# FFN chunks of 256 tokens throughout, and matmuls with unused results in TensorE's idle time

## The chip, the cores and the metric

The kernel runs on one core of a Trainium2 chip. The metric is the device time of one execution in microseconds (us). Every comparison is made against runs of the kernel before in the same rounds on the same chip.

## The reference

One transformer block on 2048 tokens of width 1024: layer norm, multi-query attention (32 heads of 32, one shared K and V), residual; layer norm, gated FFN of width 3584, residual.

```python
x = A_x
h = x + A(_layernorm(x))       # q = xn @ wq; k = xn @ wk; v = xn @ wv; softmax(q k^T / sqrt(32)) v @ wo
h2 = h + B(_layernorm(h))      # (sigmoid(hn @ w_gate) * (hn @ w_up)) @ w_down
```

## The kernel before

The program is laid out by a scheduler in Python. It holds a model of the engines' times and decides, instruction by instruction, what TensorE does next. What it decides is a fixed order: each engine is given its own list of instructions, with semaphores to wait on.

Queries are handled in 16 tiles of 128 tokens. A tile has 8 groups of 4 heads, and a group needs 8 exponentials (`exp`, 128x1024) on ScalarE, so there are 64 per tile and 1024 in all. Around them TensorE does the scores (S), the product with V (PV), the output projection (OP), and as filler, where ScalarE is busy, the FFN of an earlier tile: gate and up (GU) and down (D).

```python
CH = [[0], [1]] + [[t, t + 1] for t in range(2, NT, 2)]     # FFN chunks, in tiles: 128, 128, 256, 256, ...
NSLAB = 5                                                  # slabs of weights in flight; one slab = 256 columns of gate and of up
...
def load_slab(s, deps):
    ...
    for w, W in ((0, B_w_gate), (1, B_w_up)):
        ops.append(dma(lambda w=w, W=W: SP.dma_start(
            wgu[:, sl, w, :, :], W[:, pi * SW:(pi + 1) * SW].rearrange("(a p) f -> p a f", p=P)),
            f"sl{sl}{w}", D * SW * 2, deps, prio=4))
...
# GU of one slab: 2 x 8 matmuls for gate, as many for up, n = 128 or 256 columns each
    for f in range(2):
        for dt in range(DT):
            r.append((mm(F_ps[:, b, f * n:(f + 1) * n], wgu[:, sl, w, dt, f * P:(f + 1) * P], hnT[:, dt, 0:n],
                         dt == 0, dt == DT - 1), n, [slab_ld[s][w]] if f == dt == 0 else []))
...
    load_slab(s + NSLAB, [last])                           # after the up matmuls: both loads of a later slab
...
while True:                                                # the scheduler of TensorE
    ...                                                    # S, PV, filler groups, if one can run
    if v == 0 and known([c_id, c_w], t):                   # before the first scores: warm-up matmuls
        pl.op("pe", mm(S_ps[:, 5, :], ident[:, :], hact[:, 0:512], True, True), [c_id, c_w], **t_mm(512))
        continue
    pl.free["pe"] = t + 50.0                               # nothing to do: idle for 50 ns
    idle += 1
```

Each `matmul` becomes two instructions of TensorE, a weight load and a matmul: the profile below counts 24,252 of each.

The softmax here doesn't subtract the row's maximum and nothing guards it: scores larger than these inputs give would overflow.

## Time and profile before

| | before |
|---|---|
| median of the rounds with the change | 1208.87 us (1206.99 to 1213.16, 4 runs) |
| span of the profiled run, mean granted clock | 1204.7 us, 0.978 |
| TensorE / ScalarE busy | 94% / 87% |
| tiles 1, 2, 3 (start of the first exp to start of the next tile's) | 75.7, 72.0, 67.2 us |
| tiles 4 to 15 together | 785.3 us, so 65.4 us each |
| exps end / what is left after them | 1103.3 us / 101.4 us |

The page of the kernel before. Part 1 is busy time; in part 2 the span is cut in 40 slices of 30 us, and a digit is the busy share (or the granted clock) in tenths:

```profile
PE 1136.5 (94%) x24252; PEld 764.4 (63%) x24252; DVE 841.1 (70%) x1553; ACT 1043.2 (87%) x1202; POOL 50.6 (4%) x84
...
PE   9999889889589999999999999999999999999999
...
ACT  6799889889989999999999999999999999996010
...
PEclk9999899999679999999999999999999999999999
DMA  8764797694017551656145631656146622754470
```

The reader sees one long even stretch and a disturbed one in the slices 4 to 11, counted from 0 (120 to 360 us). The same by stretches; the columns are the stretch, its length, busy time of each engine (with instructions), granted clock, DMA share and GB/s:

```profile
130.00:200.00 70.00, 56.66 (x1507) 45.21 (x1507) 44.15 (x83) 58.93 (x73) 0.00 (x0) 0.93 0.93 261
223.00:278.00 55.00, 46.71 (x1236) 37.68 (x1237) 35.39 (x70) 45.61 (x59) 1.24 (x2) 0.97 0.94 250
300.00:342.00 42.00, 25.56 (x792) 17.81 (x782) 28.92 (x54) 38.53 (x42) 2.19 (x3) 0.66 0.07 21
345.00:1100.00 755.00, 740.58 (x16709) 501.00 (x16710) 568.88 (x1024) 729.97 (x823) 23.47 (x33) 1.00 0.49 133
```

The fourth number of busy time is ScalarE. It works 84% of the first stretch and 83% of the second, where the two FFN chunks of 128 tokens run and the DMA share is above 0.9; 92% of the third, where no FFN work is ready; and 97% of the rest. The third stretch, as TensorE's timeline shows it (start, length, what; in brackets the idle time before it and what ended it):

```profile
314.57 0.61 PE L348 MATMUL S_ps<-QTb,kT 32*128 32x128 bf16 x16 [1.43 <-ACT Pr L547]
315.12 1.90 PE L348 MATMUL F_ps<-Pr,Vb 128*32 128x128 bf16 x64
316.80 0.64 PE L348 MATMUL F_ps<-Ts,ones 128*32 128x128 bf16 x16
317.37 0.61 PE L348 MATMUL S_ps<-QTb,kT 32*128 32x128 bf16 x16
```

TensorE waits 1.43 us for ScalarE, its clock is down (0.50 from 313.2 to 326.8 us), and then the 64 PV matmuls take 1.90 us (1.08 at a clock of 1.00, at 560.77 us), so the next scores come late for ScalarE.

### The profile page before, as it was taken

The page shows a single profiled execution, that of the slowest core. Times are in us where ns is not written, and L with a number is a line of the kernel's source. Part 1 is how long each engine was busy: PE and PEld are TensorE (multiplying, and loading weights), DVE is VectorE, ACT ScalarE, POOL GpSimd, SP SyncE. Part 2 cuts the span into 40 slices and gives each one's busy share as a digit, 9 for nine tenths or more (in the row PEclk, how much of TensorE's full clock was granted, in tenths as well). Part 3 has the DMA queues.
Part 4 walks back from the last instruction along what each step waited for, and adds up shares of the span by engine and source line. Part 5 has one row for each costly group of instructions (what it writes and reads, how often), then busy time and mean ns, then how long its engine had stood idle before and what let it go on. Part 6 is the DMA issues. An engine that isn't in the chain of part 4 may idle for free.

```text
span 1204.7 us, 52525 instructions
## 1 busy us (share of the span) xinstructions
PE 1136.5 (94%) x24252; PEld 764.4 (63%) x24252; DVE 841.1 (70%) x1553; ACT 1043.2 (87%) x1202; POOL 50.6 (4%) x84
## 2 busy tenths in 40 slices
PE   9999889889589999999999999999999999999999
PEld 5745575665357765766566755766576756775684
DVE  8677667657667878687867778676877777786211
ACT  6799889889989999999999999999999999996010
POOL 4100000000000000000000000000000000000000
PEclk9999899999679999999999999999999999999999
DMA  8764797694017551656145631656146622754470
GB/s 240 195 203 141 227 277 185 167 274 99 20 48 202 151 138 35 185 143 184 43 129 142 185 101 38 187 144 174 49 123 169 179 69 68 209 144 122 123 209 18
DMA packets 315146, 172.84 MB, mean 143 GB/s; under 512 B 35120, under 2 KB 305456, under 8 KB 314928
## 3 DMA queue, kind: packets, MB, share of 16 engines
q1 hardware_dynamic: 312848, 169.37, 51.8%
q8 instruction: 190, 3.11, 1.1%
q10 hardware_dynamic: 2080, 0.13, 0.1%
q14 instruction: 28, 0.23, 0.1%
HBM read 155.32 MB, written 7.34 MB: 135 GB/s over the span
## 4 chain that ended last, share of the span: by engine, by line
PE 78%; ACT 9%; DVE 6%; issue 3%; POOL 2%; DMA 2%; POOLq 0%; DVEq 0%
PE F_ps L348 65%; PE S_ps L348 13%; ACT Pr L547 8%; DVE Ts L565 2%; DMA hnT<-hn 1%; DVE Oc L610 1%; POOL dsb L308 1%; DVE Oc L608 1%; DVE h_sb L670 1%; DVE st L289 0%; DVE st L291 0%; POOL zb L303 0%; DVE hn L317 0%; POOL rstd L310 0%; DMA zone<-ring 0%
## 5 line engine op out<-in xcount | busy, mean ns | idle before, releaser
L547 ACT ACTIVATE Pr<-S_ps 128x1024 bf16<-128x1024 f32 x1024 | 971.3, 1037 | 52.8 <-PE S_ps L348 51.9
L348 PE MATMUL F_ps<-hnT,ring 128*128 128x256 bf16 (+1 forms) x4032 | 448.1, 263 | 13.9 <-issue 4.6
L348 PEld LDWEIGHTS F_ps<-hnT,ring 128*128 128x128 bf16 x4032 | 342.8, 99 | 79.3 <-issue 19.5
L565 DVE TENSOR_TENSOR Ts<-Pr 128x1024 bf16<-128x1024 bf16 x512 | 341.2, 682 | 9.5 <-ACT Pr L547 5.5
L348 PE MATMUL S_ps<-QTb,kT 32*128 32x128 bf16 x8192 | 212.7, 220 | 31.3 <-ACT Pr L547 22.7
L348 PEld LDWEIGHTS S_ps<-QTb,kT 32*128 32x128 bf16 x8192 | 121.5, 94 | 164.0 <-ACT Pr L547 92.8
L348 PE MATMUL F_ps<-zone,hact 128*128 128x512 bf16 x896 | 218.1, 381 | 0.0
L608 DVE COPY Oc<-F_ps 128x256 f32<-128x256 f32 x128 | 54.2, 423 | 230.7 <-PE F_ps L348 230.7
L565 DVE TENSOR_TENSOR Ts<-Ts 128x1024 bf16<-128x1024 bf16 x256 | 170.5, 666 | 1.4
L348 PE MATMUL F_ps<-Pr,Vb 128*32 128x128 bf16 x8192 | 144.6, 224 | 9.5 <-issue 6.9
L348 PEld LDWEIGHTS F_ps<-Pr,Vb 128*32 128x32 bf16 x8192 | 120.5, 99 | 30.6 <-issue 12.0
L348 PEld LDWEIGHTS F_ps<-zone,hact 128*128 128x128 bf16 x896 | 78.9, 98 | 90.7 <-issue 1.1
L737 ACT ACTIVATE tnh<-F_ps 128x512 f32<-128x512 f32 (+1 forms) x126 | 70.6, 561 | 67.9 <-PE F_ps L348 67.9
L610 DVE RECIPROCAL Oc<-Oc 128x128 f32<-128x128 f32 x128 | 120.9, 945 | 0.1
L741 DVE SCALAR_TENSOR_TENSOR hact<-tnh,F_ps 128x512 bf16<-128x512 f32 (+1 forms) x126 | 77.5, 616 | 59.5 <-PE F_ps L348 57.1
L348 PE MATMUL F_ps<-zone 128*128 128x256 bf16 (+2 forms) x512 | 74.6, 289 | 3.7 <-ACT QTb L235 2.2
L348 PE MATMUL F_ps<-wo_sb,OT 128*128 128x512 bf16 x256 | 65.4, 382 | 0.7 <-DVE OT L612 0.7
L348 PE MATMUL F_ps<-Ts,ones 128*32 128x128 bf16 x2048 | 54.3, 224 | 4.3 <-issue 4.3
L303 POOL TENSOR_SCALAR zb<-mvb 128x1 bf16<-128x1 bf16 (+1 forms) x25 | 10.7, 430 | 1069.1 <-DVE mvb L299 1069.0
L348 PEld LDWEIGHTS F_ps<-zone 128*128 128x128 bf16 x512 | 38.0, 97 | 27.8 <-ACT QTb L235 3.0
L773 DVE SCALAR_TENSOR_TENSOR h_sb<-F_ps,h_sb 128x512 bf16<-128x512 f32 x32 | 21.6, 674 | 30.0 <-PE F_ps L348 29.1
L348 PEld LDWEIGHTS F_ps<-Ts,ones 128*32 128x32 bf16 x2048 | 37.0, 99 | 8.3 <-issue 8.3
(42 smaller groups left out, 275.8 us busy)
## 6 DMA issues: line engine op xcount, KB each, us to landing
ring<-in_B_w_gate_dram SPq DMA_DIRECT2D x126, 512.0 KB, 4.2
ring<-in_B_w_up_dram SPq DMA_DIRECT2D x126, 512.0 KB, 5.5
zone<-in_B_w_down_dram SPq DMA_DIRECT2D x7, 1024.0 KB, 6.9
h_sb<-in_A_x_dram SPq DMA_DIRECT2D x16, 256.0 KB, 2.8
out_dram<-h_sb SPq DMA_DIRECT2D x32, 128.0 KB, 1.7
q_scratch<-hact SPq DMA_DIRECT2D x24, 128.0 KB, 2.9
QTb<-q_scratch SPq DMA_DIRECT2D x6, 512.0 KB, 3.8
ring<-in_A_x_dram SPq DMA_DIRECT2D x5, 512.0 KB, 7.7
```

What stands on the lines that cost most here:

```text
L303: f = pl.op("pool", lambda: POOL.tensor_scalar(out=zb[:, ph, sl].unsqueeze(2), in0=mvb[:, ph, sl, 1:2], scalar1=LN_EPS_BF16, scalar2=None, ...
L308: g = pl.op("pool", lambda: POOL.tensor_tensor(out=dsb[:, ph, sl], in0=zb[:, ph, sl], in1=hb, op=ALU.pow), [f, c0], prio=prio - 1, occ=720 ...
L348: return lambda: PE.matmul(o, lhsT=l, rhs=r, start=start, stop=stop, **kw)
L547: exps[u] = pl.op("act", lambda slot=slot, pb=pb: ACT.activation(out=Pr[:, slot, :].rearrange("p (a b) -> p a b", a=2), in_=S_ps[:, pb:pb ...
L565: return pl.op("dve", lambda: DVE.tensor_tensor(out=out, in0=a, in1=b, op=ALU.add), deps, prio=prio, **t_dve(1024, 1.92))
L608: cp = pl.op("dve", lambda: DVE.tensor_copy(out=Oc[:, k, :], in_=F_ps[:, b, 0:2 * P]), [last, o_ev.get(G - 2)], prio=0, **t_dve(256))
L610: a = pl.op("dve", lambda: DVE.reciprocal(Oc[:, k, P:2 * P], Oc[:, k, P:2 * P]), [cp], prio=2, occ=880, lat=1020)
L670: h_ev[(t, dc)] = pl.op("dve", lambda: DVE.tensor_tensor(out=h_sb[:, t % 4, sl], in0=F_ps[:, b, :], in1=h_sb[:, t % 4, sl], op=ALU.add), [ ...
L737: tanh_of[s] = pl.op("act", lambda: ACT.activation(out=tnh[:, k, 0:2 * n], in_=F_ps[:, b, 0:2 * n], func=ACTF.Tanh, scale=0.5), [last, tn_ ...
L741: e = pl.op("dve", lambda: DVE.scalar_tensor_tensor(out=hactT[:, 2 * pi:2 * pi + 2, 0:n], in0=tnh[:, k, 0:2 * n].rearrange("p (a b) -> p a ...
L773: e = pl.op("dve", lambda: DVE.scalar_tensor_tensor(out=h_sb[:, t % 4, sl], in0=F_ps[:, b, :], scalar=0.5, in1=h_sb[:, t % 4, sl], op0=ALU ...
```

## The change

Its intent: one pass of the gate and up weights instead of two at the start, and no stretch at half clock (37.5 us at 0.50 between 299 and 351 us in the trace of the kernel before). Where the scheduler finds nothing to do after the first scores, it no longer lets 50 ns pass, but issues a 128x256 matmul into a PSUM bank that is free. Nobody reads the result.

```diff
-    CH = [[0], [1]] + [[t, t + 1] for t in range(2, NT, 2)]
+    CH = [[t, t + 1] for t in range(0, NT, 2)]
...
+            idle += 1
+            spare = [b for b in range(2) if known(bank_rel[b], t) and (cur is None or b != cur_b)]
+            if v and spare:
+                pl.op("pe", mm(F_ps[:, spare[0], 0:256], ident[:, :], kT4[:, 0:256], True, True), [k_ev[0]] + list(bank_rel[spare[0]]), **t_mm(256))
+                continue
             pl.free["pe"] = t + 50.0
-            idle += 1
```

## The prediction

> **What bounds the kernel now.** Two regimes, read from the busy time by window and from the starts of the 1024 exp activations (64 per 128-token tile). From 351 to 1100 us ScalarE is busy 725.5 of 749 us and TensorE 734.6: both nearly full; a pair of tiles takes about 131 us (128.6 to 133.7). Before that it is worse: tiles 1, 2, 3 take 75.7, 72.0 and 67.2 us against about 65:
> - 130.5 to 200 and 223 to 278 us: the two 128-token FFN chunks. Each streams all gate and up weights (28 loads of 512 KB) for half the tokens. The DMA share is 0.93 and 0.94 (0.50 later), TensorE waits in program order, and exps come every 1.21 and 1.25 us (1.05 in later FFN stretches, 0.93 when ScalarE alone limits).
> - 300 to 342 us: no FFN work is ready, because chunk 2 needs tiles 2 and 3. TensorE is busy 25.6 of 42 us, the granted clock falls to 0.66, exps come every 0.99 us. In the timeline ScalarE idles 0.77 us per head group, where half-clock PV matmuls (1.90 us instead of 1.08) stand before the next scores. From 342 to 351 us the clock is 0.52 and ScalarE works 7.2 of 9 us.
> - Tail: exps end at 1103 us; the last chunk runs on TensorE alone to 1204 us.
>
> [...] the throttled spans are multiples of 3.41 us at 0.5, about 51 us in all, none between 362 us and the tail.
>
> **What the change does.**
> 1. One 256-token chunk replaces two of 128: one weight pass less (14.7 MB), 448 fewer FFN matmuls with their weight loads, and 14 tanh of 0.60 us instead of 28 of 0.41 (3 us of ScalarE).
> 2. FFN work starts after tile 1 instead of tile 0. The stretch without filler moves from 300-342 us to about 130-190 us.
> 3. In that stretch TensorE has about 40% to spare, so I estimate 200 unused 128x256 matmuls at 0.115 us (17 of that form took 1.96 us). They should hold the clock at 1.0; estimated harm 0 to 2 us.
>
> **On the critical path.** Tile 0 is unchanged and ends at 103 us. By 130 us, 26 exps of tile 1 are done; the other 38 at about 0.95 us end tile 1 near 166 us, 63 us instead of 75.7: gain 12. Tiles 2 and 3 become an ordinary pair, 130.5 instead of 139.2 us: gain 9. Tiles 4 and 5 lose the throttled start: gain 2 to 3. Everything later, and the tail, only shifts. Sum 23: 1187 us, 1.9% faster, at the edge of 2%.
>
> **What would show it right.** Tile 1 ends near 166 us; no DMA share above 0.8 after 60 us; exps every 0.93 to 0.97 us from 130 to 190 us at clock 1.0; exps end near 1080 us; tail still about 101 us. Most of the gain comes from the chunks; the unused matmuls alone are worth 3 to 5 us.
>
> **What would make it wrong.** The unused matmuls delay the scores[...] (exps above 1.0 us there); the clock still drops; the static schedule falls into another order, so pairs take 128 or 134 us (7 pairs: some 20 us either way); or the tail changes, because more or less down-projection is left when exps end (25 us of it now).

What the kernel before does show is a clock of 0.66 where TensorE is busy 25.6 of 42 us, and of 1.00 where it is busy 740.6 of 755; that the unused matmuls "should hold the clock at 1.0" was the author's estimate. The sum: 12 for tile 1, 9 for tiles 2 and 3, 2 to 3 for tiles 4 and 5, so 23.

## More of the kernel before

The same kernel differs by some us from chip to chip: the kernel before had medians of 1203.4, 1205.6 and 1208.9 us in the jobs below. So ratios within a job are what counts, and a few us between jobs mean nothing.

## The result, and the profile after

The changed kernel took 1194.62 us (1193.29 to 1198.72, 4 runs) against 1208.87 us: ratio 0.9883, 95% interval 0.9847 to 0.9919. All ratios here are the mean time of one kernel's fast runs over that of the other's of the same rounds, so not quite the ratio of the medians quoted. In a second job, with 6 runs, it was 0.9872 (0.9844 to 0.9900). It is 14 to 16 us faster; the prediction was 23.

The page of the changed kernel, the same lines:

```profile
PE 1138.6 (95%) x24020; PEld 775.2 (65%) x24141; DVE 843.1 (71%) x1539; ACT 1041.8 (87%) x1188; POOL 50.4 (4%) x84
...
PE   8899899999999999999998899999999999999998
...
ACT  6799899999998999999998999999999999995110
...
PEclk9999999999999999999999999999999999999999
DMA  8765501665155632655054652656155723654470
```

(This trace lacks 121 matmul records, 24,020 against 24,141 weight loads.) The low clock is gone but for two spells of 3.41 us in the trace, at 147.9 and 369.8 us. But the row of ScalarE is not clean: there are eights in slices 12 and 21 (counted from 0), where before had nines. The stretches of the changed kernel:

```profile
130.00:150.00 20.00, 16.76 (x389) 12.26 (x382) 12.52 (x23) 16.26 (x19) 0.00 (x0) 0.95 0.67 232
150.00:190.00 40.00, 39.79 (x940) 29.26 (x941) 27.63 (x49) 38.92 (x43) 0.00 (x0) 0.98 0.05 16
190.00:320.00 130.00, 127.28 (x2996) 88.96 (x3008) 99.80 (x182) 128.51 (x146) 3.54 (x6) 1.00 0.48 129
320.00:1088.00 768.00, 733.47 (x16696) 503.85 (x16770) 577.84 (x1034) 734.11 (x826) 26.02 (x36) 1.00 0.49 132
```

From 150 to 320 us ScalarE works 97 to 99% of the time: this is what was hoped for. From 320 to 1088 us it works 95.6%, where the kernel before had 96.7%. By tiles:

| us | before | after | predicted |
|---|---|---|---|
| tile 1 ends | 178.7 | 170.7 | 166 |
| tile 3 ends | 318.0 | 298.4 | about 296.5 |
| tiles 4 to 15 | 785.3 | 792.9 | about 783 |
| exps end | 1103.3 | 1091.3 | about 1080 |
| after the exps | 101.4 | 101.5 | 101 |

At the end of tile 3 the gain is 19.6 us. Then 7.6 us are given back in tiles 4 to 15, although the work there is the same and the prediction had "Everything later, and the tail, only shifts". The views of waits tell of what kind the loss is. The columns are the engine that waited, what ended the wait, us in total, times, longest us. Before, from 130 to 280 us:

```profile
...
DVE Oc L608 <- PE F_ps L348: 32.6, 15, 4.0
ACT Pr L547 <- PE S_ps L348: 18.6, 19, 2.5
PEld F_ps L348 <- issue: 13.5, 20, 2.5
...
PEld S_ps L348 <- issue: 10.9, 12, 2.3
```

After, from 300 to 1088 us:

```profile
...
PEld S_ps L348 <- issue: 49.6, 189, 2.1
ACT Pr L547 <- PE S_ps L348: 33.0, 53, 2.1
PEld F_ps L348 <- issue: 21.9, 45, 2.2
```

"Issue" means that TensorE stood still and waited for nothing that the profile shows. Most of those waits are short, but a few are of 2 us, and no DMA of weights is on the list in either kernel. One of them in the timeline of the changed kernel:

```profile
367.20 0.39 PE L348 MATMUL F_ps<-hnT,ring 128*128 128x256 bf16 x2
...
367.52 0.40 PE L348 MATMUL S_ps<-QTb,kT 32*128 32x128 bf16 x14
...
369.86 0.29 PE L348 MATMUL S_ps<-QTb,kT 32*128 32x128 bf16 x2 [1.94 <-issue]
...
370.18 1.02 ACT L547 ACTIVATE Pr<-S_ps 128x1024 bf16<-128x1024 f32 x1 [2.13 <-PE S_ps L348]
```

The gap stands inside one block of 16 score matmuls, after the fourteenth. Nothing in the program waits there. ScalarE loses 2.13 us by it, and right after, from 369.8 us on, the clock is at half for 3.41 us.

**What these gaps are.** The trace also has the DMA queue that brings instructions: 189 packets of 16,384 bytes (190 in the kernel before), about as many as TensorE's stream has blocks of 256 instructions: its 48,577 instructions (48,826 before) make 189.8 such blocks (190.7). I call such a block a page. I counted TensorE's instructions in the trace (a pair for each weight load, 24,141 of them, and 295 of semaphores and drains; 24,252 and 322 before) up to each gap over 0.9 us between 130 us and the last exp, from the start of one instruction to that of the next, and looked at what the instruction queue had done:

```
gaps over 0.9 us, 130 us to the last exp     before   after   after, second job
  all                                          30       11       11
  at position 193 or 194 modulo 256            12       10       10      (19.9, 15.6, 14.6 us)
page k starts with packet k-1 landed 1.2 to 1.7 us before (both kernels; the starts with a gap above 0.7 us)
```

Most of the others of the kernel before are waits for ScalarE from 295 to 345 us. So TensorE stands still where its stream crosses from one page of 256 instructions to the next and the page has landed only 1.2 to 1.7 us before. Counting pages and packets, packet k-1 (from 0) was always the one that had just landed when page k started with such a gap, and it had begun to move after page k-1 had started: about one page is fetched ahead. In tiles 4 to 15 of the changed kernel a page lasts 5.8 us on average (3.7 us the shortest), the packet begins to move 1.56 us after the start of the page before (3.8 us at most), it takes 1.13 us (median), and some 1.4 us more pass before TensorE goes on. The sum of the means is 4.1 us, that of the worst case is 6.3 us, more than a page lasts.

By these gaps the two kernels differ as follows (TensorE idle for more than 0.25 us right before position 193 or 194, from one profile each; some expectations below quote other counts of the same gaps): tiles 1 to 3, 16.0 us before and 3.2 after; tiles 4 to 15, 9.7 before and 17.2 after. The last difference, 7.5 us, is the size of the 7.6 us given back. Both vary with the profile: in the second job's profile of the changed kernel, tiles 4 to 15 have 13.6 us of such gaps and take 787.5 us. That is a correlation, and the experiments have to make it a cause.

### The profile page after: what moved, and what is told of

Read it like the earlier page. It is cut to its first block, busy times and chain, and to the rows that moved or that the text cites. A ratio compares the mean times of both kernels' runs of the same rounds, so it can differ in the third digit from the quotient of the medians.

```text
span 1192.8 us, 52074 instructions
## 1 busy us (share of the span) xinstructions
PE 1138.6 (95%) x24020; PEld 775.2 (65%) x24141; DVE 843.1 (71%) x1539; ACT 1041.8 (87%) x1188; POOL 50.4 (4%) x84
## 4 chain that ended last, share of the span: by engine, by line
PE 83%; ACT 6%; DVE 5%; issue 4%; DMA 1%; POOL 1%; SPq 0%; DVEq 0%
PE F_ps L348 70%; PE S_ps L348 13%; ACT Pr L547 5%; DVE Ts L565 1%; DMA hnT<-hn 1%; DVE st L289 1%; DVE st L291 1%; POOL dsb L308 0%; DMA ring<-in_A_x_dram 0%; DVE Oc L610 0%; DVE Oc L608 0%; DVE ring L328 0%; POOL zb L303 0%; ACT ring L332 0%; POOL rstd L310 0%
## 5 line engine op out<-in xcount | busy, mean ns | idle before, releaser
L348 PE MATMUL F_ps<-hnT,ring 128*128 128x256 bf16 x3584 | 441.8, 274 | 9.3 <-issue 4.4
L348 PEld LDWEIGHTS F_ps<-hnT,ring 128*128 128x128 bf16 x3584 | 330.7, 98 | 76.4 <-issue 12.3
L348 PE MATMUL F_ps<-zone,hact 128*128 128x512 bf16 x822 | 199.5, 380 | 6.2 <-issue 5.3
L348 PE MATMUL F_ps<-Pr,Vb 128*32 128x128 bf16 x8192 | 138.7, 220 | 2.1 <-issue 1.3
L348 PEld LDWEIGHTS F_ps<-Pr,Vb 128*32 128x32 bf16 x8192 | 115.8, 97 | 25.1 <-issue 8.1
L737 ACT ACTIVATE tnh<-F_ps 128x512 f32<-128x512 f32 x112 | 67.6, 603 | 65.0 <-PE F_ps L348 64.8
L741 DVE SCALAR_TENSOR_TENSOR hact<-tnh,F_ps 128x512 bf16<-128x512 f32 x112 | 76.0, 678 | 54.7 <-PE F_ps L348 53.5
L348 PE MATMUL F_ps<-zone 128*128 128x256 bf16 (+2 forms) x497 | 71.1, 287 | 5.9 <-ACT QTb L235 2.2
L348 PE MATMUL F_ps<-wo_sb,OT 128*128 128x512 bf16 x227 | 58.7, 381 | 3.1 <-issue 2.5
L348 PE MATMUL F_ps<-kT,ident 128*128 128x256 bf16 x337 | 43.9, 279 | 0.0
```

What stands on the lines that cost most here:

```text
L348: return lambda: PE.matmul(o, lhsT=l, rhs=r, start=start, stop=stop, **kw)
L737: tanh_of[s] = pl.op("act", lambda: ACT.activation(out=tnh[:, k, 0:2 * n], in_=F_ps[:, b, 0:2 * n], func=ACTF.Tanh, scale=0.5), [last, tn_ ...
L741: e = pl.op("dve", lambda: DVE.scalar_tensor_tensor(out=hactT[:, 2 * pi:2 * pi + 2, 0:n], in0=tnh[:, k, 0:2 * n].rearrange("p (a b) -> p a ...
```

## The experiments

**Theory.** A page fetch that waits behind bursts of weight loads comes late, and TensorE stalls. The two small chunks were slow by this, and the change, which shifts every later instruction to another place in its page, met more such stalls in the second part. **Rivals:** TensorE waits for the weights themselves (so the prediction); the unused matmuls get in the way; the new static order is worse.

All 12 runs, with numbers from each run's timed rounds (first three columns) and from its profile (the rest: tiles in us; mean wait from a page's start to the next packet's start in tiles 4 to 15, us; idle time of TensorE above 0.25 us at page starts there, us):

| run | median us | before, same job | ratio (95%) | tiles 1-3 | tiles 4-15 | fetch wait | page gaps |
|---|---|---|---|---|---|---|---|
| before | 1208.87 | | | 214.9 | 785.3 | 1.41 | 9.7 |
| after | 1194.62 | 1208.87 | 0.9883 (0.9847-0.9919) | 195.5 | 792.9 | 1.56 | 17.2 |
| e0_after_again | 1189.89 | 1205.60 | 0.9872 (0.9844-0.9900) | 194.1 | 787.5 | 1.48 | 13.6 |
| e1_chunks_only | 1193.09 | 1203.42 | 0.9910 (0.9865-0.9956) | 205.8 | 783.5 | 1.26 | 8.4 |
| e2_unused_only | 1199.56 | 1203.42 | 0.9978 (0.9930-1.0025) | 207.7 | 780.2 | 1.40 | 8.7 |
| e3_shift_after | 1195.10 | 1203.42 | 0.9929 (0.9882-0.9976) | 196.5 | 785.3 | 1.17 | 12.2 |
| e4_loads_cut_after | 1168.64 | 1203.42 | 0.9715 (0.9676-0.9754) | 195.2 | 767.4 | 0.52 | 0.0 |
| e5_unread_before | 1202.31 | 1205.60 | 0.9970 (0.9928-1.0013) | 210.4 | 785.1 | 1.06 | 6.4 |
| e6_split4_after | 1170.71 | 1205.60 | 0.9710 (0.9684-0.9737) | 195.4 | 767.8 | 0.86 | 0.0 |
| e7_paced_after | 1172.38 | 1205.60 | 0.9729 (0.9702-0.9756) | 194.5 | 771.9 | 1.04 | 1.4 |
| e8_before_split4 | 1184.69 | 1208.93 | 0.9805 (0.9784-0.9826) | 205.7 | 773.0 | 0.85 | 0.4 |
| e8_chunks_split4 | 1172.88 | 1208.93 | 0.9709 (0.9690-0.9729) | 198.1 | 768.9 | 0.89 | 0.5 |
| e8_unused_split4 | 1178.18 | 1208.93 | 0.9758 (0.9733-0.9783) | 203.9 | 767.0 | 0.86 | 0.0 |
| e9_split_all | 1169.49 | 1208.93 | 0.9681 (0.9660-0.9702) | 192.2 | 768.0 | 0.90 | 0.0 |

All results are correct but those of e4 and e5.

### The two halves alone

```diff
 # e1_chunks_only: the kernel before with
-    CH = [[0], [1]] + [[t, t + 1] for t in range(2, NT, 2)]
+    CH = [[t, t + 1] for t in range(0, NT, 2)]
 # e2_unused_only: the changed kernel with the old CH
```

> The chunks of 256 tokens without the unused matmuls. If the chunks bring most of the gain and the unused matmuls only hold the clock (prediction): 1196 to 1200 us, 3 to 5 us above the changed kernel (1194.6); from 150 to 190 us the granted clock drops below 0.8 and exps come every 0.97 to 1.0 us; tile 1 ends near 174 us. If the unused matmuls cost more than they bring (rival for the missing 8 us of the prediction): 1187 to 1193 us. If the loss is TensorE waiting for its own instructions at page boundaries: tiles 4 to 15 differ from the 792.8 us of the changed kernel by a few us either way, by as much as their page stalls differ.

> The old chunks with the unused matmuls. Prediction: 1203 to 1206 us, that is 3 to 5 us under before, all of it from 300 to 351 us, where the clock stays near 1.0 and exps come every 0.93 to 0.96 us instead of 0.99. The stretches 130-200 and 223-278 us stay slow (exps every 1.2 us, DMA share above 0.9). If the unused matmuls delay the scores: no gain or slower than 1209 us.

Measured: chunks alone 0.9910, unused matmuls alone 0.9978 (its interval includes 1). The stretches of the chunks alone show what the unused matmuls do:

```profile
130.00:150.00 20.00, 9.91 (x365) 7.08 (x366) 13.78 (x25) 19.23 (x22) 0.00 (x0) 0.71 0.67 232
150.00:190.00 40.00, 23.89 (x704) 15.73 (x696) 26.00 (x46) 35.59 (x39) 0.00 (x0) 0.71 0.04 15
190.00:200.00 10.00, 6.83 (x154) 4.90 (x155) 8.00 (x17) 8.70 (x10) 2.19 (x3) 0.50 0.15 28
```

From 150 to 190 us the clock is 0.71 (0.98 with them), and an exp comes every 1.05 us (0.929 with them). So they do hold the clock. Yet in tiles 4 to 15 this run is 9.4 us faster than the changed kernel, with 8.8 us less of page gaps. As a time, e1's 1193.1 us is at the edge of what was expected for "unused matmuls cost"; but the kernel before was 5 us faster on this chip than in the first job, and the ratio 0.9910, about 1198 us there, is what was expected for "chunks bring most". In e2 the clock from 300 to 351 us is 1.00 and an exp comes every 0.97 us (1.04 before), nearly as expected; but tiles 1 and 2 gained too, which was not. The intervals of about 1% are too wide to tell the two halves apart here. Page stalls are part of the noise (13.6 and 17.2 us in tiles 4 to 15 of the two profiles of the changed kernel), and the square below takes most of it away.

### The same plan, with the pages shifted

```diff
+ # e3_shift_after: the first 21 warm-up matmuls are issued as 4 of 128 columns instead of one of 512
+            def four():
+                for i in range(4):
+                    r = PE.matmul(S_ps[:, 5, i * P:(i + 1) * P], lhsT=ident[:, :], rhs=hact[:, i * P:(i + 1) * P], start=True, stop=True)
```

> The changed kernel; 21 of the warm-up matmuls of 512 columns at the start are each cut into 4 of 128, so that every later TensorE instruction stands 126 places later in its stream; plan and order are the same. Theory (TensorE stalls where it crosses a 256-instruction page whose fetch is late): the long gaps again lie at one and the same position modulo 256 (193 or 194), but at other matmuls and times; the sum of tiles 4 to 15 changes from 792.8 us by 2 to 8 us either way, by as much as the page stalls (25.9 us in them now) change. Rival (the static order of the larger chunks, or the unused matmuls, cost the 8 us): tiles 4 to 15 stay at 792 to 794 us and the time at 1194 to 1196 us.

All page gaps over 0.9 us of this run lie at times where the changed kernel had none of that length (206, 223, 242, 276, 396, 415, 881, 902 and 936 us here, and two of just 0.9 us at 1025 and 1060 us; 139, 144, 351, 368, 424, 610 to 683 us in the changed kernel), and all are at position 193 or 194 of the page again. The order of work is the same (but for the cut warm-ups), so the gaps belong to the place in the instruction stream and not to what is computed there. In the profiled run tiles 4 to 15 took 785.3 us instead of 792.9, with 5.0 us less of page gaps. As a time it is inconclusive: that profiled run (1189.7 us) was the fastest of its four, the median of 1195.1 us is what the rival had named (on a chip where the kernel before was 5 us faster), and the ratio, 0.9929, is no better than that of the changed kernel. So e3 shows where the gaps fall, not what they cost. The changed kernel run again (e0) has its gaps where it had them: 139, 144, 366, 419, 605, 623, 642, 660 and 677 us; only the one at 351 us fell below 0.9 us, and one at 523 us is new.

> The changed kernel itself, as the neighbour of the other runs on this chip. Ratio to before 0.985 to 0.992. Theory of page stalls: at every gap above 0.9 us after 130 us TensorE's position in its stream is 193 or 194 modulo 256, and the gap ends 1.2 to 1.6 us after an instruction packet landed.

Met but for one gap: 10 of 11 lie at 193 or 194. The eleventh, at 459 us, is at position 90 in both profiles of this kernel, and is no page start.

### Without the weights' traffic, and without the wait for it

```diff
 # e4_loads_cut_after: after the first five slabs, an eighth of each load (wrong results on purpose)
-                    wgu[:, sl, w, :, :], W[:, pi * SW:(pi + 1) * SW]...
+                    wgu[:, sl, w, 0:(DT if s < NSLAB else 1), :], W[0:(D if s < NSLAB else P), pi * SW:(pi + 1) * SW]...
 # e5_unread_before: the kernel before; the loads run as ever, but the matmuls read another tile and don't wait (wrong results on purpose)
+  deps = list(deps) + slab_ld.get(s - NSLAB, [])                               # in load_slab: after the load that used the slab before
-  mm(F_ps[...], wgu[:, sl, w, dt, f * P:(f + 1) * P], hnT[:, dt, 0:n], ...)
+  mm(F_ps[...], wo_sb[:, dt, (2 * w + f) * P:(2 * w + f + 1) * P], hnT[:, dt, 0:n], ...)
+  if e == "pe" and d.key is not None and d.key.startswith("sl"): continue      # no wait for a slab
```

> The changed kernel with wrong results on purpose: after the first five slabs every gate and up load brings one eighth of its rows, so the DMA traffic falls to a fraction; TensorE's stream and the waits are the same. Theory (instruction fetches wait behind weight loads): the wait from the start of a page to the start of the next page's fetch falls from 1.6 us (mean, 320 to 1088 us) to below 0.8, gaps above 0.7 us at page boundaries vanish after 200 us, tiles 4 to 15 take 768 to 778 us instead of 792.8, total 1170 to 1180 us. Rival (TensorE or ScalarE limit alone, whatever the DMA does): 1190 us or more.

> The kernel before with wrong results on purpose: the gate and up matmuls read their weights from a tile that was loaded long before (the output projection), and TensorE does not wait for the slab loads; the same loads still run, unread. The prediction said that in the two 128-token chunks TensorE waits for the streamed weights: then those stretches get as fast as other FFN work, exps every 1.05 us, tiles 1 to 3 take about 196 us instead of 214.9, total 15 to 20 us below before. Theory of page stalls (the loads delay TensorE's instruction fetches): no change, tiles 1 to 3 take 210 to 217 us, page gaps of 12 to 18 us in them, total within 5 us of before.

With the traffic gone (e4) the mean fetch wait is 0.52 us, no page gap above 0.25 us is left in tiles 4 to 15 (17.2 us in the changed kernel), and these tiles take 767.4 us, 25.5 less. That is 8 us more than the gaps themselves; what the rest is stays open. The whole kernel takes 1168.6 us. TensorE's stream and its waits are the same, and so is ScalarE's work, which now fills 98% of the stretch:

```profile
320.00:1064.00 744.00, 740.99 (x16823) 502.20 (x16812) 576.83 (x1036) 732.54 (x828) 26.01 (x36) 1.00 0.12 33
```

The two page gaps over 0.9 us that are left stand at 139 and 144 us, while loads of the down weights and the first slabs, which this run did not cut, are moving.

With the wait gone but the traffic kept (e5) nothing much happens: 0.9970, tiles 1 to 3 take 210.4 us instead of 214.9, and gaps of about 2 us at page starts go on (156, 231, 242 and 270 us). (The edit also takes 247 waits out of TensorE's stream, so its pages begin at other places.) The second small chunk in that run still leaves ScalarE idle:

```profile
130.00:200.00 70.00, 57.69 (x1572) 44.84 (x1576) 48.37 (x93) 63.35 (x78) 2.07 (x3) 0.98 1.02 280
223.00:278.00 55.00, 46.84 (x1172) 35.49 (x1177) 37.62 (x73) 45.76 (x58) 2.12 (x3) 0.97 1.06 268
```

ScalarE works 45.76 us of the 55, where it had 45.61 before. The prediction's step "TensorE waits in program order" for the streamed weights is refuted as the main cause: with no such wait in the program the second stretch is as slow. The first chunk gained 4.4 us of ScalarE time; whether that was a wait for weights or another fall of the page stalls is open.

### The same bytes in smaller bursts

```diff
 # e6_split4_after: four loads of 128 KB in place of one of 512 KB
+                for h in range(4):
+                    o = dma(lambda w=w, W=W, h=h: SP.dma_start(wgu[:, sl, w, h * 2:(h + 1) * 2, :], W[h * 2 * P:(h + 1) * 2 * P, ...]...
+                ops.append(o)
 # e7_paced_after: after the gate matmuls the next gate load, after the up matmuls the next up load
+                    load_slab(s + NSLAB, [last], (0,))
-                load_slab(s + NSLAB, [last])
+                load_slab(s + NSLAB, [last], (1,))
```

> The changed kernel with every gate and up load cut into 4 loads of 128 KB, issued one after the other; TensorE's stream is the same. If a fetch waits only for the packet of the one load that is being moved, the wait before a fetch (1.56 us mean in tiles 4 to 15) falls to about 0.8 us and tiles 4 to 15 from 792.9 to about 775 us; total ratio to before 0.97 to 0.98. If it waits for everything that is queued ahead: mean wait stays 1.3 to 1.7 us, time within 3 us of the changed kernel. If SyncE's issuing becomes the limit: slower.

> The changed kernel, where the next gate load is issued when the gate matmuls are done and the next up load when the up matmuls are done, instead of both together; TensorE's stream is the same. Theory (a fetch waits behind what was queued on its DMA engine): the longest waits (3.8 us) fall to about 2 us, the mean in tiles 4 to 15 from 1.56 to 1.0-1.3 us, most gaps above 0.7 us vanish, tiles 4 to 15 take 774 to 784 us instead of 792.9, the ratio to before 0.975 to 0.983. If the fetch wait does not depend on how the loads bunch: no change from the changed kernel.

In both, TensorE's order is that of the changed kernel. Cut in four, the fetch wait falls from 1.48 us (the neighbour e0) to 0.86, the page gaps from 13.6 us to none, and the time from 1189.9 to 1170.7 us. Issued apart, 1.04 us, 1.4 us and 1172.4 us. The same stretch of the changed kernel and, below it, of the cut loads:

```profile
320.00:1064.00 744.00, 710.30 (x16155) 487.62 (x16227) 560.61 (x1004) 710.80 (x800) 26.02 (x36) 1.00 0.48 130
```

```profile
320.00:1064.00 744.00, 728.07 (x16766) 502.60 (x16834) 576.82 (x1037) 732.37 (x827) 26.02 (x36) 1.00 0.50 136
```

And how the gate loads were issued in the two kernels, in the view of the DMAs (how many, KB each, median us from issue to landing):

```profile
ring<-in_B_w_gate_dram SPq DMA_DIRECT2D x112, 512.0 KB, 4.1
```

```profile
ring<-in_B_w_gate_dram SPq DMA_DIRECT2D x448, 128.0 KB, 2.5
```

In the same 744 us, ScalarE does 827 instructions instead of 800, while the DMA share and the GB/s are even a little higher (0.50 for 0.48, 136 for 130). So not the amount of traffic hurts, but how it is bunched when a fetch comes. By what mechanism a fetch waits behind loads is not shown by these runs. By the trace a load of 512 KB is 1024 pieces of 512 bytes of 27 ns (median); spread evenly over the 16 DMA engines that the profile counts that is an estimated 64 x 27 ns = 1.7 us each. The longest measured waits are longer than that: the ten longest fetch waits of tiles 4 to 15, 3.4 to 3.8 us in the changed kernel and 3.4 to 4.0 us in e0, ended within 0.35 us of the end of a burst of load packets (packets that start less than 0.15 us apart), as if the fetch had waited for all that was queued. In e6 the longest was 2.4 us.

Cutting the loads also spreads them, because SyncE takes its time for each issue (0.37 and 0.58 us for one load, 2.74 and 2.01 us for four). A pair of gate and up loads as it is issued in the changed kernel and, below it, cut in four (start, length, what):

```profile
481.00 0.37 SPq L711 DMA_DIRECT2D ring<-in_B_w_gate_dram  x1
481.42 0.58 SPq L711 DMA_DIRECT2D ring<-in_B_w_up_dram  x1
```

```profile
480.91 2.74 SPq L712 DMA_DIRECT2D ring<-in_B_w_gate_dram  x4
483.69 2.01 SPq L712 DMA_DIRECT2D ring<-in_B_w_up_dram  x4
```

The same megabyte is issued over 4.8 us instead of 1.0. So e6 does not tell smaller loads from loads that are spread out; that was not tested apart. The longest wait of e7 was still 3.6 us, so the rule by which a fetch gets its turn, of which the expectations of e6 and e7 name possible ones, is not settled here.

### The square, with page stalls nearly gone

The same cut was made in the kernel before and in the two halves. In the kernels with old chunks the scheduler then orders a few groups differently, so those are not the same stream as their neighbours without the cut.

> The kernel before (chunks of 128 at the start, no unused matmuls) with every gate and up load cut into 4 of 128 KB. Theory: the page gaps (16.1 us in tiles 1 to 3, 9.5 us in tiles 4 to 15) mostly go, ratio to before 0.980 to 0.987; in tiles 1 to 3 some gaps stay, since the DMA share there is above 0.9. If the two small chunks were slow because TensorE waits for the weights' volume: tiles 1 to 3 stay above 208 us.

> Chunks of 256 tokens, no unused matmuls, loads cut into 4. Beside the changed kernel with cut loads (ratio 0.971) it shows what the unused matmuls are worth when page stalls do not blur it. Prediction's 3 to 5 us: ratio 0.974 to 0.977; clock below 0.8 from 150 to 190 us. If they are worth nothing: 0.969 to 0.972.

> Old chunks with unused matmuls, loads cut into 4. With the other three it completes the square: if chunks and unused matmuls add up, its ratio is that of the kernel before with cut loads less about 0.004 (5 us), so 0.976 to 0.983.

| loads cut in four, ratio to before | no unused matmuls | unused matmuls |
|---|---|---|
| old chunks | 0.9805 (1184.7 us) | 0.9758 (1178.2 us) |
| new chunks | 0.9709 (1172.9 us) | 0.9710 (1170.7 us, the other job) |

Here the runs of one kernel agree within 0.3%. The chunks are worth 11.8 us. The unused matmuls are worth 6.5 us with the old chunks, and between 0 and 2 us on top of the new ones. The profiles say why so little: without them tile 2 takes 68.4 us, with them 64.0 (the clock: 0.71 and 1.00 from 150 to 190 us, 0.50 and 1.00 from 190 to 200); but tile 1 takes 65.7 without and 67.3 with them: with them a page is used up sooner (1329 matmuls from 130 to 190 us, 1069 without), and a gap of 2.4 us at 145 us is there, which the run without them does not have. So the two halves do not add up: 11.8 and 6.5 us alone, about 14 us together. They hold the clock, and they eat instructions. The old chunks with cut loads keep 205.7 us in tiles 1 to 3, against 195.4: even there only part was page stalls, and the rest is what the new chunks bring.

### What beats both

```diff
 # e9_split_all: e6, and the 7 loads of the down weights (1 MB) in 4 of 256 KB
+            for k in range(f, f + n):
+                o = dma(lambda k=k: SP.dma_start(wd_sb[:, k, :], B_w_down[k * P:(k + 1) * P, :]), f"wd{f}", P * D * 2, deps, prio=4)
```

> The changed kernel with cut gate and up loads, and also the seven down-projection loads of 1 MB cut into 4 of 256 KB. The last large page gaps (0.9 and 2.6 us at 139 and 144 us, while those loads run) shrink below 0.5 us: tile 1 takes 63 to 65 us instead of 67.3, total 2 to 4 us below the 1170.7 us of the cut gate and up loads alone, ratio 0.967 to 0.970.

0.9681, 1169.49 us, 39 us below the kernel before and the best ratio of all; tile 1 takes 63.8 us, and one page gap of 1.2 us is left, where less than 0.5 us was expected. Against e6 the ratios' intervals touch (0.9684 and 0.9702), so the last step is shown in the profile and not surely in the time.

## Why the prediction was right or wrong

The measured 1194.6 us is 7.6 us above the 1187 us of the prediction: the gain was 14 us instead of 23. That it came so near is in part luck, since the gain of the first tiles, 19.6 us where 21 were predicted, came, going by the page gaps in the traces, mostly by another mechanism than the predicted one.

- **The 128-token chunks: "Each streams all gate and up weights", "TensorE waits in program order": wrong in its mechanism.** Without that wait (e5) the second stretch stays as slow. Twelve gaps over 0.9 us at page starts, 19.9 us together, lie in the kernel before, nine of them, 16.4 us, from 139 to 259 us. The gain of the stretch was right by size: of the 19.4 us that tiles 1 to 3 gained, 12.8 are page gaps (16.0 us before, 3.2 after); the rest is not itemised. With the loads cut in the kernel before (e8_before_split4) these gaps fell to 5.0 us, and tiles 1 to 3 from 214.9 to 205.7 us.
- **"Tile 1 ends near 166 us": 170.7 us.** From 150 to 190 us exps come every 0.929 us at a clock of 0.98, as predicted, but gaps of 0.9 and 2.6 us at page starts at 139 and 144 us, while down weights are loaded, cost most of the rest. With those loads cut (e9), tile 1 takes 63.8 us, and the prediction said 63.
- **"Tiles 2 and 3 become an ordinary pair", 130.5 us: better, 127.8 us.** They had no page gap above 0.25 us. The "ordinary" 131 us contained some.
- **"Tiles 4 and 5 lose the throttled start: gain 2 to 3. Everything later, and the tail, only shifts": this is the step that failed.** Tile 4 did gain 3.3 us (66.8 to 63.5), but tile 5 lost 5.8 (64.1 to 69.9), and tiles 4 to 15 together became 7.6 us slower in the profile. The 337 unused matmuls and the 448 missing FFN matmuls move every later instruction to another place in its page, and the page gaps there went from 9.7 to 17.2 us (13.6 in e0). That these gaps are caused by fetches late behind loads is shown by e4, e6 and e7; that the place decides where they fall, by e3. That the increase, and not a decrease, came with this change is chance of the position, as far as the runs show.
- **"Unused matmuls alone are worth 3 to 5 us":** 6.5 us with old chunks, 0 to 2 us on top of new chunks, both with cut loads. The estimate, from TensorE's time to spare alone, missed that they also use up pages.
- **"They should hold the clock at 1.0":** 0.98 from 150 to 190 us, and 0.71 there without them (e1). What makes the clock drop is not shown. In the kernel before it was at half for 37.5 us between 299 and 351 us, and TensorE's longest idle gap between matmuls from 297 to 351 us was 1.43 us. In the changed kernel a page gap of 2.1 us at 367.7 us was followed at once by 3.41 us at half clock, in one profile; in the other profile of the same kernel gaps of 1.6 and 2.4 us were not.
- **"No DMA share above 0.8 after 60 us":** held, in stretches of 20 us, until the tail, where the last chunk has it at 0.95 (1.08 before).
- **Tail 101 us:** 101.5 us.

The prediction named a shift of some 20 us either way from the static order as a risk. A shift came, but not from the order of work: in e3, e4, e6 and e7 TensorE's order of work is that of the changed kernel, and the ratio to before goes from 0.993 to 0.971.

## What to carry to other kernels

This long, fully unrolled kernel streamed its own instructions by DMA: every 5.8 us a page of 16 KB, with 4.1 us (the sum of the means) to 6.3 us (of the worst) from the start of one page until the next could run. If, as here, an engine "waits for nothing" for 1 to 2 us inside a block of identical instructions, count its instructions modulo 256, and look at what loads were queued. Cutting 512 KB loads into 128 KB, or issuing them apart, was worth 1.5 to 1.6% here without moving a byte less, more than the change that was studied. And the filler instructions were not free, although the engine had idled there: they use up pages (337 pairs here, so about 2.6 pages), and with cut loads tile 1 took 67.3 us with them and 65.7 us without.
